# Weight conversion queued behind each attention step, with a fixed order of the first transfers

## The chip, the cores and the metric

The kernel runs on one core of one Trainium2 chip. A core has a matrix engine (PE), three engines that work on vectors (DVE, ACT and POOL), and a queue, SP, that issues transfers (DMAs) between the chip's memory and the on-chip buffers. Each engine takes its instructions strictly in the order in which they stand in its own queue; engines wait for one another by semaphores. The metric is the device time of one execution in microseconds (us), the median of three.

## The reference

Three parts are computed in sequence, all in float32:

```
k_all, v_all = concat(k_g, k_l), concat(v_g, v_l)          # per batch (4) and head (8): 32 global + 512 local rows of 64
out_g = softmax(q_g @ k_all.T / 8) @ v_all
a_l   = softmax(concat(q_l @ k_g.T / 8, where(|i - j| <= 32, q_l @ k_l.T / 8, -1e9)))
out_l = a_l @ concat(v_g, v_l)
x = concat(out_g, out_l) as 2304 tokens x 512
x = x / sqrt(mean(x * x) + 1e-6) * rms_g
x = (silu(x @ w_gate) * (x @ w_val)) @ w_out               # 512 -> 1536 -> 512
h = x @ w_in                                               # 512 -> 2048
out = ((a0 + a1 h + a2 h^2 + a3 h^3) / (1 + |b0||h| + |b1| h^2 + 1e-6)) @ w_out2   # 2048 -> 512
```

The weights arrive as 64-bit floats, which the engines do not compute in.

## The kernel before

**Weights.** A weight tile (512 columns by 128 rows, 512 KB as 64-bit words) is loaded by one DMA (line 66) and turned into two float32 tiles, a rounded high part and the rest, by eight instructions in four stages (`Weights.stages`): ACT at lines 83 and 85, DVE at lines 91, 92 and 95, POOL at line 99, then ACT at line 104 and POOL at line 105. `Weights.step` moves each tile under way by one stage and takes up a new one when fewer than two are under way. The gate, value and output tiles of the first group (g0 to g3, v0 to v3, o0 to o3) are converted while attention runs.

**Attention** runs in 32 steps, one per batch, pair of heads and half of the 512 rows. Step s transposes keys (`make_k`, tile psK) and queries (`make_q`, psQ), multiplies them (`scores`, psS), takes mask and minimum on DVE (tile p), exponentiates on ACT (line 367, tile p), transposes (psT), multiplies with the values (`pv`, psO) and transposes back (psX) into the token tile x. The windows of values, vw, are laid out by two loads from memory and two copies from buffer to buffer (line 278). Keys, queries and values of a step are loaded two to four steps ahead, into buffers that are used in turn (kin0, kin1, qin0, qin1, vw0 to vw3). Every fourth step or so handles the global rows as well (psG, psGT, psOg).

**The first feed-forward block** follows in *units* of 12 matmuls (tiles psg, psv, psA), spread among the attention steps: from step `START` a target of units per step is set, at first 7 units up to step `SECOND`, then up to 60 at the last step. Before a group of tokens is used it is normalized (`norm`, tiles st and x) and split (tile xt).

**What sets the order.** The code is traced in the loop over t in `tile_attn_ffn_kernel`; a scheduler then puts the instructions of each engine in an order from priorities and a model of their times. `tc.issue_after(i)` keeps what is traced inside it behind instruction i on i's engine. Transfers on SP carry one of eight semaphores in turn, so that a DMA is issued when the one eight places ahead has landed.

**In the first five steps** of before, `wts.step` is called four times per t from t = 2. The order in which its instructions and those of attention stand is left to the scheduler. One small instruction belongs to the last part of the kernel: line 918 takes the absolute value of the coefficients b (tile bv) on ACT, and its DMA is issued at t = 3.

Of the kernel before, what the change touches and what calls it, by code (L numbers as in the profile page):

```python
# [134 lines left out]
class Attention:  # L135
# [9 lines left out]
    def __init__(self, tc, pool, x, q_l, k_l, v_l, q_g, k_g, v_g, more):  # L145
        self.tc, self.nc, self.pool, self.x = tc, tc.nc, pool, x
        self.q_l, self.k_l, self.v_l, self.q_g, self.k_g, self.v_g = q_l, k_l, v_l, q_g, k_g, v_g
        nc = self.nc
        self.kin = [pool.tile([128, 4, 2, D], F32, name=f"kin{i}") for i in range(2)]
        self.qin = [pool.tile([128, 2, 2, D], F32, name=f"qin{i}") for i in range(2)]  # L150
        self.gin = pool.tile([128, 2, 2, D], F32, name="gin")
# [22 lines left out]
        self.load_v(0)  # L174
        NEG = -8.0e9
        self.masks = []
        for v in (1, 2, 0):
            m = pool.tile([128, 128], F32, name=f"mask{v}")
            nc.gpsimd.memset(m, 0.0)
            for j in range(4):  # L180
                lo = m[32 * j : 32 * j + 32, 0:96]
                nc.gpsimd.affine_select(
                    out=lo, in_=lo, compare_op=ALU.is_ge, fill=NEG, base=0, pattern=[[1, 96]], channel_multiplier=-1
                )
                nc.gpsimd.affine_select(
                    out=lo, in_=lo, compare_op=ALU.is_ge, fill=NEG, base=2 * WIN, pattern=[[-1, 96]], channel_multiplier=1
                )
            if v == 0:
                nc.gpsimd.memset(m[0:32, 0:32], NEG)
            if v == 2:  # L190
                nc.gpsimd.memset(m[96:128, 64:96], NEG)
            self.masks.append(m)
        self.masks = [self.masks[2], self.masks[0], self.masks[1]]
# [12 lines left out]
        self.load_v(3)  # L206
        self.load_g(0, 1, nc.sync)
# [26 lines left out]

    def load_q(self, s):
        b, hp, u = self.place(s)
        src = self.q_l[b, 2 * hp : 2 * hp + 2, 256 * u : 256 * u + 256]
        if b == 0:
            self.nc.sync.dma_start(
# [3 lines left out]
        else:  # L243
            for hf in range(2):
                self.nc.sync.dma_start(out=self.qin[s % 2][:, :, hf], in_=src[hf].rearrange("(n p) d -> p n d", p=128))

    def load_g(self, b, i, eng):

        g = (self.k_g, self.q_g)[i]
        for hp in range(4):  # L250
            eng.dma_start(
                out=self.gin[32 * hp : 32 * hp + 32, i], in_=g[b, 2 * hp : 2 * hp + 2].rearrange("h j d -> j h d")
            )

    def load_v(self, s):
# [7 lines left out]
        dma = self.nc.sync.dma_start  # L263
# [13 lines left out]
        for p0, w0 in ((0, 0), (64, 2)):  # L277
            dma(out=t[p0 : p0 + 32, :, 1:9], in_=t[32:64, :, w0 : w0 + 8])
# [7 lines left out]

    def load_vn(self, r):
# [3 lines left out]
        self.nc.sync.dma_start(  # L291
# [3 lines left out]
        self.nc.sync.dma_start(out=t[0:32, :, 4], in_=self.v_g[b, 2 * hp : 2 * hp + 2].rearrange("h j d -> j h d"))  # L295
# [30 lines left out]
    def make_g(self, b, i):  # L326
        nc, ps = self.nc, self.bank(1, f"psKG{b}_{i}")
        nc.tensor.transpose(ps[:, 0:128], self.gin[:, i].rearrange("p h d -> p (h d)"), self.ident)
        if i == 0:
            nc.vector.tensor_copy(self.kgt[b % 2], ps[:, 0:128].rearrange("d (p j) -> d p j", p=4))  # L330
            return
        for hf in range(2):
            rows = slice(64 * hf, 64 * hf + 64)
            nc.vector.tensor_copy(
                self.qgz[b % 2][rows, :, 32 * hf : 32 * hf + 32], ps[rows, 0:128].rearrange("d (p j) -> d p j", p=4)
            )

    def scores(self, s):
# [27 lines left out]
        for i in range(4):  # L366
            nc.scalar.activation(out=p[:, i], in_=p[:, i], func=AF.Exp, scale=-1.0, bias=nm[:, i : i + 1])
# [109 lines left out]
    def step(self, t, between):  # L477
# [3 lines left out]
        if t < NS:  # L481
            if i == 0:
# [274 lines left out]
def kernel(  # L757
# [73 lines left out]
    START, SECOND, IN_ATTN = 5, 11, 60  # L831
# [4 lines left out]
    att.set_pools(pp, banks, apool, (3, 2))  # L836
# [5 lines left out]
    for t in range(LAST + 1):  # L842
# [20 lines left out]
        if t >= 2:  # L863
            for _ in range(4 if t < 6 else 2):
# [93 lines left out]
```

## Time and profile before

| | us |
|---|---|
| median of three runs | 1089.58 (1089.46 to 1092.65) |
| the profiled execution | 1092.84 |
| its span, first to last instruction | 1091.1 |
| PE busy in the span | 1007.9 (92%) |
| DVE busy | 792.8 (73%) |
| ACT busy | 600.2 (55%) |
| POOL busy | 373.4 (34%) |

A table of stretches gives the busy time of each engine in each stretch of the span; the difference to its length is the engine's idle time. A list of waits gives, for an engine, what ended its idle time, summed. In a timeline a row has start, duration, engine, line, operation and tiles, and in brackets the idle time ahead of it with what ended it. SPq rows are the issue of DMAs. The page's 40 slices show the granted PE clock below its full value in the first tenth of the span.

### The profile page before, as it was taken

Reading aid. Unit: us, or ns where it says so; the run is one execution under the profiler, and the core shown is the slowest. Engines: PE = TensorE matmul, PEld = TensorE weight load, DVE = VectorE, ACT = ScalarE, POOL = GpSimd, SP = SyncE. Lnnn points to the kernel's source line nnn. Section 1 sums busy time; section 2 is a strip of 40 time slices with the busy share of each in tenths; the row PEclk is TensorE's granted clock in tenths of the full one; section 3 lists DMA queues with packets and bytes.
Section 4 is the critical chain, followed back from the end, with each engine's and each line's share of the span. In section 5 each row is a group of like instructions: output and inputs, shape, how many; then the busy total and the mean of one; then the engine's idle time right before and its main releaser. Section 6 shows DMA issues by size and latency. Waiting matters only on the chain.

```text
span 1091.1 us, 23781 instructions
## 1 busy us (share of the span) xinstructions
PE 1007.9 (92%) x9368; PEld 907.3 (83%) x9368; DVE 792.8 (73%) x1750; ACT 600.2 (55%) x1347; POOL 373.4 (34%) x421
## 2 busy tenths in 40 slices
PE   3669898998989989999999999999999999999997
PEld 2547777877778889899989999888989989898895
DVE  4674554655529999873797453599898998989987
ACT  3644545645447675552654342466666666666675
POOL 5461212212135743220231111354343543435433
PEclk7669999999999999999999999999999999999999
DMA  7943544434116330650430113500000000000000
GB/s 161 276 127 84 114 123 98 108 100 105 32 39 253 117 116 20 212 174 2 155 117 8 33 40 87 185 1 1 30 1 20 11 1 30 1 30 1 1 31 20
DMA packets 104432, 83.46 MB, mean 76 GB/s; under 512 B 63744, under 2 KB 91392, under 8 KB 104320
## 3 DMA queue, kind: packets, MB, share of 16 engines
q1 hardware_dynamic: 102592, 75.64, 23.8%
q0 software_dynamic: 1728, 6.29, 1.8%
q8 instruction: 74, 1.21, 0.5%
q14 instruction: 38, 0.31, 0.1%
HBM read 62.64 MB, written 10.75 MB: 67 GB/s over the span
## 4 chain that ended last, share of the span: by engine, by line
PE 50%; DVE 29%; ACT 8%; DMA 4%; issue 4%; POOL 3%; SPq 2%; ACTq 0%; POOLq 0%; DVEq 0%
PE psg L606 3%; PE psg L608 3%; DVE q L725 3%; PE psS L349 3%; PE psv L608 3%; DVE q L713 3%; PE psv L607 3%; PE psH L703 3%; PE psH L704 3%; PE psv L606 3%; PE psg L607 3%; PE psH L705 3%; PE psB L738 3%; PE psA L633 3%; PE psB L739 3%
## 5 line engine op out<-in xcount | busy, mean ns | idle before, releaser
L130 POOL TENSOR_SCALAR gh<-p 128x384 fp32r<-128x384 f32 (+1 forms) x96 | 58.1, 605 | 210.2 <-DVE p L727 185.8
L703 PE MATMUL psH<-yt,w_h 128*128 128x384 f32 (+1 forms) x384 | 126.0, 329 | 0.9 <-ACT yt L685 0.7
L704 PE MATMUL psH<-yt,w_h 128*128 128x384 f32 (+1 forms) x384 | 125.4, 327 | 0.0
L705 PE MATMUL psH<-yt,w_h 128*128 128x384 f32 (+1 forms) x384 | 123.5, 328 | 0.9 <-DVE yt L686 0.9
L606 PE MATMUL psg<-xt,w_g 128*128 128x288 f32 (+1 forms) x384 | 114.8, 300 | 7.9 <-ACT xt L595 7.9
L633 PE MATMUL psA<-ah,w_o 128*128 128x288 f32 (+1 forms) x384 | 114.3, 299 | 7.6 <-ACT ah L622 3.8
L608 PE MATMUL psg<-xt,w_g 128*128 128x288 f32 (+1 forms) x384 | 114.2, 299 | 5.3 <-DVE xt L596 4.4
L606 PE MATMUL psv<-xt,w_v 128*128 128x288 f32 (+1 forms) x384 | 112.7, 294 | 1.2 <-DVE a L620 1.1
L738 PE MATMUL psB<-w_p,gh 128*128 128x512 f32 x272 | 108.4, 398 | 5.5 <-POOL gh L130 5.4
L607 PE MATMUL psv<-xt,w_v 128*128 128x288 f32 (+1 forms) x384 | 112.0, 292 | 0.0
L635 PE MATMUL psA<-al,w_o 128*128 128x288 f32 (+1 forms) x384 | 111.5, 291 | 0.5 <-DVE al L624 0.4
L608 PE MATMUL psv<-xt,w_v 128*128 128x288 f32 (+1 forms) x384 | 111.8, 292 | 0.0
L634 PE MATMUL psA<-ah,w_o 128*128 128x288 f32 (+1 forms) x384 | 111.6, 291 | 0.0
L607 PE MATMUL psg<-xt,w_g 128*128 128x288 f32 (+1 forms) x384 | 111.5, 291 | 0.0
L729 POOL TENSOR_TENSOR gl<-p,gh 128x384 fp32r<-128x384 f32 (+1 forms) x96 | 108.6, 1131 | 8.0
L739 PE MATMUL psB<-w_p,gh 128*128 128x512 f32 x272 | 107.2, 394 | 0.0
L723 ACT ACTIVATE r<-q,cq 128x384 f32<-128x384 f32 (+1 forms) x96 | 57.4, 598 | 63.4 <-DVE q L713 62.4
L713 DVE SCALAR_TENSOR_TENSOR q<-q,bv,t 128x384 f32<-128x384 f32 (+1 forms) x96 | 68.8, 717 | 21.7 <-ACT q L711 21.6
L621 DVE SCALAR_TENSOR_TENSOR a<-a,psv 128x256 f32<-128x256 f32 (+1 forms) x96 | 41.6, 434 | 56.5 <-ACT a L617 48.2
L606 PEld LDWEIGHTS psg<-xt,w_g 128*128 128x128 f32 x384 | 73.3, 191 | 10.7 <-ACT xt L595 8.9
L633 PEld LDWEIGHTS psA<-ah,w_o 128*128 128x128 f32 x384 | 73.3, 191 | 10.5 <-ACT ah L622 4.5
L740 PE MATMUL psB<-w_p,gl 128*128 128x512 f32 x272 | 82.1, 395 | 0.0
(173 smaller groups left out, 2815.5 us busy)
## 6 DMA issues: line engine op xcount, KB each, us to landing
vw<-vw SPq DMA_DIRECT2D x64, 130.0 KB, 2.5
raw_h<-in_moe_w_in_dram SPq DMA_DIRECT2D x16, 512.0 KB, 3.8
raw_p<-in_moe_w_out_dram SPq DMA_DIRECT2D x16, 512.0 KB, 4.6
raw_g<-in_moe_w_gate_dram SPq DMA_DIRECT2D x12, 512.0 KB, 4.6
raw_v<-in_moe_w_val_dram SPq DMA_DIRECT2D x12, 512.0 KB, 5.9
raw_o<-in_moe_w_out_dram SPq DMA_DIRECT2D x12, 512.0 KB, 6.8
vw<-in_v_l_dram SPq DMA_DIRECT2D x62, 80.0 KB, 2.5
out_dram<-o SPq DMA_DIRECT2D x17, 256.0 KB, 2.0
```

The source lines that it names most:

```text
L606: nc.tensor.matmul(ps, wh, xt[c][:, 0], start=(c == 0), stop=False)
L607: nc.tensor.matmul(ps, wl, xt[c][:, 0], start=False, stop=False)
L608: nc.tensor.matmul(ps, wh, xt[c][:, 1], start=False, stop=(c == 3))
L633: nc.tensor.matmul(ps, wh, ah, start=(i == 0), stop=False)
L634: nc.tensor.matmul(ps, wl, ah, start=False, stop=False)
L635: nc.tensor.matmul(ps, wh, al, start=False, stop=(i == 3))
L703: nc.tensor.matmul(ph[:, :n], wh, yt[:, c, 0, :n], start=(c == 0), stop=False)
L704: nc.tensor.matmul(ph[:, :n], wl, yt[:, c, 0, :n], start=False, stop=False)
L705: nc.tensor.matmul(ph[:, :n], wh, yt[:, c, 1, :n], start=False, stop=(c == 3))
L729: nc.gpsimd.tensor_tensor(out=gl[:, :n], in0=p, in1=gh[:, :n].bitcast(F32), op=ALU.subtract)
L738: nc.tensor.matmul(acc[m], gh[:, sl], wh, start=(k == 0), stop=False)
L739: nc.tensor.matmul(acc[m], gh[:, sl], wl, start=False, stop=False)
```

## The change

- `wts.step` is called 0, 1, 2, 2, 3, 3, 3, 3 times in steps 0 to 7, then twice per step, and in steps 0 to 7 what it issues on ACT and DVE stands behind that step's last exponential and last mask instruction.
- The DMAs that attention issues through `self.dma` are chained in the order of the code in steps 0 to 7. Keys and queries of step 1 and the first weight tile move ahead, the copies of the value windows (`spread_v`) are issued apart from their loads, and the eight small loads of global keys and queries per batch become two.
- One mask is selected on POOL, and the other two are copied from it on DVE.
- `make_g` does global keys and queries in one go, after the queries of the batch's first step.
- Step 8 drains steps 4 to 7 stage by stage, as step 4 does with steps 0 to 3. `SECOND` goes from 11 to 9, the second normalization from t = 10 to t = 8, and the p tile has two buffers for three.

```diff
+        self.order_dma = True
+        self.last_dma = self.last_ttr = self.last_exp = None
         self.load_k(0)
         self.load_q(0)
-        self.load_g(0, 0, nc.sync)
-        make_identity(nc, self.ident)
+        self.load_g(0)
         nc.vector.memset(self.vw[0], 1.0)
         nc.vector.memset(self.vw[1], 1.0)
+        self.load_v(0)
+        self.load_k(1)
+        self.load_q(1)
+        more()
+        self.spread_v(0)
+        self.load_v(1)
+        more()
+        self.spread_v(1)
+        make_identity(nc, self.ident)
...
-        for v in (1, 2, 0):
+        for v in range(3):
             m = pool.tile([128, 128], F32, name=f"mask{v}")
...
+        for v, p0, c0 in ((2, 96, 64), (0, 0, 0)):
+            nc.vector.tensor_copy(self.masks[v], m)
+            nc.vector.memset(self.masks[v][p0 : p0 + 32, c0 : c0 + 32], NEG)
...
-        self.load_k(1)
-        self.load_q(1)
-        self.load_v(1)
-        more()
-        more()
         self.load_v(2)
         self.load_v(3)
-        self.load_g(0, 1, nc.sync)
+
+    def dma(self, out, in_):
+
+        with self.tc.issue_after(self.last_dma.ins) if self.last_dma else nullcontext():
+            d = self.nc.sync.dma_start(out=out, in_=in_)
+        if self.order_dma:
+            self.last_dma = d
...
+    def spread_v(self, s):
+        t = self.vw[s % 4]
+        for p0, w0 in ((0, 0), (64, 2)):
+            self.dma(out=t[p0 : p0 + 32, :, 1:9], in_=t[32:64, :, w0 : w0 + 8])
...
         if t < NS:
-            if i == 0:
-                self.make_g(b, 0)
             if i < 4:
                 self.make_k(4 * b + i)
-            if i == 4:
-                self.make_g(b, 1)
             self.make_q(t)
-        if t == 4:
+            if i == 0:
+                self.make_g(b)
+        if t >= 8:
+            self.order_dma = False
+        if 3 <= t < NS:
+            self.spread_v(t + 1) if t + 1 < NS else None
+        elif t in (0, 1):
+            self.spread_v(t + 2)
+        if t in (4, 8):
             for to in (2, 3, 4):
-                for s in range(4):
+                for s in range(t - 4, t):
                     self.advance(s, to)
+                    between()
...
-    START, SECOND, IN_ATTN = 5, 11, 60
+    START, SECOND, IN_ATTN = 5, 9, 60
...
-    att.set_pools(pp, banks, apool, (3, 2))
+    att.set_pools(pp, banks, apool, (2, 2))
...
-        if t % 4 == 2 and t > 8:
+        if t % 4 == 2 and t > 12:
             norms.append(ffn.norm(ORD[(t - 6) // 4]))
-        elif t == 4:
-            norms.append(ffn.norm(ORD[0]))
+        elif t in (4, 8):
+            norms.append(ffn.norm(ORD[t // 4 - 1]))
...
-        if t >= 2:
-            for _ in range(4 if t < 6 else 2):
+        with ExitStack() as late:
+            if t < 8:
+                late.enter_context(tc.issue_after(att.last_exp.ins))
+                late.enter_context(tc.issue_after(att.last_ttr.ins))
+            for _ in range((0, 1, 2, 2, 3, 3, 3, 3)[t] if t < 8 else 2):
                 wts.step(nc.gpsimd)
```

**Place 1, SP, up to the second load into kin0.** These are the keys of step 2 (raw_g and raw_v are weight tiles; a row with x2 is two DMAs). Before:

```order
L66 DMA raw_g_0_235<-in_moe_w_gate_dram 128x4x256
L278 DMA vw1_101<-vw1_101 32x2x520 x2
L66 DMA raw_v_0_237<-in_moe_w_val_dram 128x4x256
L266 DMA vw2_102<-in_v_l_dram 32x10x64 x2
L282 DMA vw2_102<-in_v_g_dram 32x8x64 x2
L266 DMA vw3_103<-in_v_l_dram 32x10x64 x2
L282 DMA vw3_103<-in_v_g_dram 32x8x64 x2
L278 DMA vw2_102<-vw2_102 32x2x520 x2
L278 DMA vw3_103<-vw3_103 32x2x520 x2
L251 DMA gin_91<-in_q_g_dram 32x2x64 x4
L227 DMA kin0_87<-in_k_l_dram 128x2x256
```

The same place of the change:

```order
L66 DMA raw_g_0_125<-in_moe_w_gate_dram 128x4x256
L214 DMA vw0_100<-vw0_100 32x2x520 x2
L214 DMA vw1_101<-in_v_l_dram 32x10x64 x2
L214 DMA vw1_101<-in_v_g_dram 32x8x64 x2
L66 DMA raw_v_0_133<-in_moe_w_val_dram 128x4x256
L66 DMA raw_g_1_280<-in_moe_w_gate_dram 128x4x256
L214 DMA vw1_101<-vw1_101 32x2x520 x2
L214 DMA vw2_102<-in_v_l_dram 32x10x64 x2
L214 DMA vw2_102<-in_v_g_dram 32x8x64 x2
L214 DMA vw3_103<-in_v_l_dram 32x10x64 x2
L214 DMA vw3_103<-in_v_g_dram 32x8x64 x2
L214 DMA kin0_87<-in_k_l_dram 128x2x256
```

The keys of step 2 were the 39th DMA of the program and are the 30th. The copies of vw2 and vw3 and the query half of gin no longer stand ahead of them, one more weight tile does. The DMA of bv was the 58th and is the 50th.

**Place 2, ACT, ahead of the exponentials of step 3 (p3).** cv, raw and w are weight tiles in conversion, qt and pt attention's own. Before:

```order
L322 ACTIVATE qt3_540<-psQ3_539 128x256
L85 ACTIVATE raw_g_3_503<-raw_g_3_503 128x512
L85 ACTIVATE raw_v_3_505<-raw_v_3_505 128x512
L374 ACTIVATE pt2_552<-psT2_547 128x512
L104 ACTIVATE w_g_2_842<-cv4_652 128x512
L918 ACTIVATE bv_83<-bv_83 128x2
L104 ACTIVATE w_v_2_849<-cv5_661 128x512
L85 ACTIVATE raw_o_0_631<-raw_o_0_631 128x512
L83 ACTIVATE cv6_846<-raw_g_3_503 128x512
L85 ACTIVATE raw_o_1_633<-raw_o_1_633 128x512
L367 ACTIVATE p3_588<-p3_588,nm_108 128x128 x2
L405 ACTIVATE x0_0_70<-psX0_624 128x256
```

The same place of the change:

```order
L83 ACTIVATE cv1_462<-raw_v_0_133 128x512
L85 ACTIVATE raw_v_0_133<-raw_v_0_133 128x512
L331 ACTIVATE qt3_482<-psQ3_481 128x256
L382 ACTIVATE pt2_496<-psT2_491 128x512
L933 ACTIVATE bv_83<-bv_83 128x2
L375 ACTIVATE p3_532<-p3_532,nm_108 128x128 x2
L413 ACTIVATE x0_0_70<-psX0_566 128x256
L375 ACTIVATE p3_532<-p3_532,nm_108 128x128 x2
L104 ACTIVATE w_g_0_577<-cv0_359 128x512
```

The seven conversion instructions between qt3 and p3 are gone from there; the instruction on bv still stands ahead of p3.

**Place 3, DVE, between the masks of step 5 and of step 6** (a1 is the first feed-forward unit's activation, gm the global rows' maximum). Before:

```order
L620 SCALAR_TENSOR_TENSOR a1_0_960<-a1_0_960,psg_1_0_889 128x256
L621 SCALAR_TENSOR_TENSOR a1_0_960<-a1_0_960,psv_1_0_890 128x256
L420 TENSOR_REDUCE gm_110<-psG1_0_978 128x1
L467 COPY x0_0_70<-psGX0_1144 64x2x32 x2
L421 TENSOR_REDUCE gm_110<-psG1_1_979 128x1
L422 TENSOR_REDUCE gm_110<-gm_110 128x1
L423 TENSOR_SCALAR gm_110<-gm_110 128x1
```

The same place of the change:

```order
L91 TENSOR_SCALAR cv5_772<-cv5_772 128x512
L92 TENSOR_SCALAR cv5_772<-cv5_772 128x512
L95 SCALAR_TENSOR_TENSOR cv5_772<-raw_v_2_357,cv5_772 128x512
L632 SCALAR_TENSOR_TENSOR a1_0_875<-a1_0_875,psg_1_0_804 128x256
L633 SCALAR_TENSOR_TENSOR a1_0_875<-a1_0_875,psv_1_0_805 128x256
L428 TENSOR_REDUCE gm_110<-psG1_0_893 128x1
L91 TENSOR_SCALAR cv6_913<-cv6_913 128x512
L475 COPY x0_0_70<-psGX0_1072 64x2x32 x2
L429 TENSOR_REDUCE gm_110<-psG1_1_894 128x1
L92 TENSOR_SCALAR cv6_913<-cv6_913 128x512
L430 TENSOR_REDUCE gm_110<-gm_110 128x1
L95 SCALAR_TENSOR_TENSOR cv6_913<-raw_g_3_455,cv6_913 128x512
```

Before, all twelve tiles (cv0 to cv11) have passed DVE ahead of the masks of step 5; in the change five have (cv0 to cv4), and seven stand among steps 5 to 8 and the first units.

## Rows read from the trace of the kernel before

**Rows 1.** Table of stretches: busy us per engine, granted clock, DMA share, GB/s
```profile
core 0: us, PE busy (x) PEld busy (x) DVE busy (x) ACT busy (x) POOL busy (x), PEclk, DMA share, GB/s
0.00:28.30 28.30, 9.99 (x213) 7.87 (x213) 11.76 (x40) 8.58 (x18) 16.06 (x48) 0.79 0.73 164
28.30:50.70 22.40, 13.37 (x260) 10.89 (x261) 13.91 (x39) 15.17 (x33) 10.21 (x8) 0.65 0.97 283
50.70:76.70 26.00, 15.76 (x214) 10.07 (x213) 20.86 (x51) 14.11 (x35) 16.78 (x14) 0.63 0.59 156
80.00:130.00 50.00, 44.51 (x871) 36.26 (x871) 25.59 (x113) 24.90 (x69) 9.86 (x13) 0.96 0.43 100
130.00:1091.00 961.00, 920.93 (x7778) 839.22 (x7777) 719.46 (x1507) 535.89 (x1191) 317.25 (x335) 0.99 0.21 66
```

**Rows 2.** Waits of PE, whole span: us in total, times, longest
```profile
PE psg L606 <- ACT xt L595: 7.9, 5, 5.1
PE psT L372 <- ACT p L367: 6.7, 1, 6.7
PE psK L304 <- DMA kin<-in_k_l_dram: 5.3, 2, 4.9
PE psQ L304 <- issue: 4.3, 1, 4.3
```

**Rows 3.** Timeline, single rows from 0 to 77 us
```profile
0.74 0.44 SPq L227 DMA_DIRECT2D kin<-in_k_l_dram  x1
...
16.56 0.66 ACT L83 ACTIVATE cv<-raw_g 128x512 f32<-128x512 f32 x1 [7.75 <-DMA raw_g<-in_moe_w_gate_dram]
...
25.38 0.38 SPq L227 DMA_DIRECT2D kin<-in_k_l_dram  x1
...
28.33 1.98 PE L304 MATMUL psK<-ident,kin 128*64 128x128 f32 x16 [4.92 <-DMA kin<-in_k_l_dram]
...
40.08 1.23 SPq L781 DMA_DIRECT2D bv<-in_moe_b_dram  x1
...
44.82 0.19 ACT L918 ACTIVATE bv<-bv 128x2 f32<-128x2 f32 x1
...
50.31 0.39 ACT L367 ACTIVATE p<-p,nm 128x128 f32<-128x128 f32 x1
...
76.70 0.58 PE L606 MATMUL psg<-xt,w_g 128*128 128x256 f32 x1 [5.05 <-ACT xt L595]
```

**Rows 4.** Groups of ACT instructions, 28.3 to 50.7: count, busy us, mean ns
```profile
L367 ACT ACTIVATE p<-p,nm 128x128 f32<-128x128 f32 x8 | 2.8, 389 | 0.0
L85 ACT ACTIVATE raw_g<-raw_g 128x512 int32<-128x512 uint32 x3 | 2.0, 675 | 0.4 <-DMA raw_g<-in_moe_w_gate_dram 0.4
...
L83 ACT ACTIVATE cv<-raw_v 128x512 f32<-128x512 f32 x3 | 2.0, 663 | 0.3 <-DMA raw_v<-in_moe_w_val_dram 0.2
...
L104 ACT ACTIVATE w_g<-cv 128x512 fp32r<-128x512 f32 x2 | 1.2, 623 | 0.0
```

**Rows 5.** Groups of DVE instructions, 50.7 to 76.7
```profile
L91 DVE TENSOR_SCALAR cv<-cv 128x512 f32<-128x512 f32 x5 | 4.1, 818 | 3.4 <-ACT cv L83 3.4
L92 DVE TENSOR_SCALAR cv<-cv 128x512 int32<-128x512 int32 x5 | 3.9, 781 | 0.1
L95 DVE SCALAR_TENSOR_TENSOR cv<-raw_o,cv 128x512 int32<-128x512 int32 x4 | 3.2, 804 | 0.0
```

**Rows 6.** Single lines, 0 to 90 us: ns min/median/max of one instruction
```profile
L91 DVE TENSOR_SCALAR cv<-cv x12: 415/490/1460, 17.2 to 72.4; 128x512 f32<-128x512 f32 x12
...
L92 DVE TENSOR_SCALAR cv<-cv x12: 411/427/1397, 18.4 to 73.1; 128x512 int32<-128x512 int32 x12
...
L95 DVE SCALAR_TENSOR_TENSOR cv<-raw_g,cv x4: 682/693/694, 18.9 to 50.0; 128x512 int32<-128x512 int32 x4
L95 DVE SCALAR_TENSOR_TENSOR cv<-raw_v,cv x4: 676/1180/1779, 21.9 to 52.9; 128x512 int32<-128x512 int32 x4
```

More of the change, by code (lines that the diff above doesn't have):

```diff
@@ L150, in __init__ @@
         self.qin = [pool.tile([128, 2, 2, D], F32, name=f"qin{i}") for i in range(2)]
-        self.gin = pool.tile([128, 2, 2, D], F32, name="gin")
+        self.gin = pool.tile([64, 2 * 4, D], F32, name="gin")
         self.kt = [pool.tile([128, 576], F32, name=f"kt{i}") for i in range(4)]
@@ L173, in __init__ @@
             nc.vector.memset(z, 0.0)
-        self.load_v(0)
         NEG = -8.0e9
         self.masks = []
-        for v in (1, 2, 0):
+        for v in range(3):
             m = pool.tile([128, 128], F32, name=f"mask{v}")
[L179 to L191, printed above, removed]
-            self.masks.append(m)
-        self.masks = [self.masks[2], self.masks[0], self.masks[1]]
+            self.masks.append(m)
+        m = self.masks[1]
+        nc.gpsimd.memset(m, 0.0)
+        for j in range(4):
+            lo = m[32 * j : 32 * j + 32, 0:96]
+            nc.gpsimd.affine_select(
+                out=lo, in_=lo, compare_op=ALU.is_ge, fill=NEG, base=0, pattern=[[1, 96]], channel_multiplier=-1
+            )
+            nc.gpsimd.affine_select(
+                out=lo, in_=lo, compare_op=ALU.is_ge, fill=NEG, base=2 * WIN, pattern=[[-1, 96]], channel_multiplier=1
+            )
+        for v, p0, c0 in ((2, 96, 64), (0, 0, 0)):
+            nc.vector.tensor_copy(self.masks[v], m)
+            nc.vector.memset(self.masks[v][p0 : p0 + 32, c0 : c0 + 32], NEG)
         for vw in self.vw[2:]:
@@ L226, in load_k @@
         if b == 0:
-            self.nc.sync.dma_start(
+            self.dma(
                 out=self.kin[r % 2].rearrange("p n h d -> p (n h d)").rearrange("p (h f) -> p h f", h=2),
@@ L238, in load_q @@
         if b == 0:
-            self.nc.sync.dma_start(
+            self.dma(
                 out=self.qin[s % 2].rearrange("p n h d -> p (n h d)").rearrange("p (h f) -> p h f", h=2),
@@ L244, in load_q, with load_g @@
             for hf in range(2):
[L245 to L253, printed above, removed]
+                self.dma(out=self.qin[s % 2][:, :, hf], in_=src[hf].rearrange("(n p) d -> p n d", p=128))
+    def load_g(self, b):
+        for i, g in enumerate((self.k_g, self.q_g)):
+            self.dma(out=self.gin[32 * i : 32 * i + 32], in_=g[b].rearrange("h j d -> j h d"))
     def load_v(self, s):
@@ L262, in load_v @@
         v = self.v_l[b, 2 * hp]
-        dma = self.nc.sync.dma_start
+        dma = self.dma
         def cut(h0, h1, w0, w1):
@@ L290, in load_vn @@
         t = self.vn[r % 3]
-        self.nc.sync.dma_start(
+        self.dma(
             out=t[:, :, 0:4].rearrange("p h n d -> p h (n d)"),
@@ L324, in make_q, with make_g @@
             self.load_q(s + 2)
-    def make_g(self, b, i):
-        nc, ps = self.nc, self.bank(1, f"psKG{b}_{i}")
-        nc.tensor.transpose(ps[:, 0:128], self.gin[:, i].rearrange("p h d -> p (h d)"), self.ident)
-        if i == 0:
-            nc.vector.tensor_copy(self.kgt[b % 2], ps[:, 0:128].rearrange("d (p j) -> d p j", p=4))
-            return
+    def make_g(self, b):
+        nc, ps = self.nc, self.bank(1, f"psKG{b}")
+        for p in range(4):
+            src = self.gin[:, 2 * p : 2 * p + 2].rearrange("p h d -> p (h d)")
+            nc.tensor.transpose(ps[:, 64 * p : 64 * p + 64], src, self.ident[0:64, 0:64])
+        v = ps[:, 0:256].rearrange("d (p i j) -> d i p j", p=4, i=2)
+        nc.vector.tensor_copy(self.kgt[b % 2], v[:, 0])
         for hf in range(2):
             rows = slice(64 * hf, 64 * hf + 64)
-            nc.vector.tensor_copy(
-                self.qgz[b % 2][rows, :, 32 * hf : 32 * hf + 32], ps[rows, 0:128].rearrange("d (p j) -> d p j", p=4)
-            )
+            nc.vector.tensor_copy(self.qgz[b % 2][rows, :, 32 * hf : 32 * hf + 32], v[rows, 1])
     def scores(self, s):
@@ L366, in scores @@
         for i in range(4):
-            nc.scalar.activation(out=p[:, i], in_=p[:, i], func=AF.Exp, scale=-1.0, bias=nm[:, i : i + 1])
+            self.last_exp = nc.scalar.activation(out=p[:, i], in_=p[:, i], func=AF.Exp, scale=-1.0, bias=nm[:, i : i + 1])
     def trans(self, s):
@@ L496, in step @@
         if t < NS and i == 4 and b + 1 < B:
-            for j in range(2):
-                self.load_g(b + 1, j, self.nc.sync)
+            self.load_g(b + 1)
         if t < NS and i in (3, 4, 5):
```

9 lines of the change are left out of this document (3 added, 6 removed).

## The prediction

> **What bounds the kernel now.** I read the table of stretches first. In 961 us from 130 us on PE is busy for 920.93, with its clock at 0.99 [rows 1]: there the kernel goes at PE's pace. Up to the first feed-forward matmul at 76.70 us [rows 3] PE is busy for 9.99 + 13.37 + 15.76 = 39.1 us and idle for 37.6 [rows 1]. This change works on that beginning. If the first unit comes earlier with the same attention steps done, all that follows can move up by as much, since the later loads are placed by the work ahead of them, not by the time.
>
> The waits of PE name what fills the idle time [rows 2]: the exponentials of step 0, the keys of step 2, a wait of 4.3 us put down to nothing, and the split tokens of the first unit. The timeline shows what is behind them [rows 3]. ACT stood still for 7.75 us in front of a conversion whose weight tile had not landed, with the first exponentials queued behind. The keys of step 2 were issued only at 25.38 us, and PE took them at 28.33. The last exponential of step 3 began at 50.31, and ended at 50.7.
>
> **The change, part by part.** I follow the path to the first unit in three terms, and price the conversions that are put off as a fourth.
>
> *A, the keys of step 2.* The first DMA was issued at 0.74 us and the 39th, these keys, at 25.38 [rows 3]: 38 issues in 24.6 us, 0.65 us each. The change has 29 ahead of them, so 9 x 0.65 = 5.8 us are saved: issue at 19.5, and with the same 2.95 us to their use, 22.5 for 28.33. The transfer engines were at a share of 0.73 in this stretch and 0.97 in the next [rows 1], so there is room for a faster issue. Bounds: no gain, if the bytes ahead (much the same) set the pace, to 5.8. I take 5.8, since the share lies well under the next stretch's. That the exponentials of step 0 no longer wait for a weight tile is worth nothing by itself: steps 0 and 1 then end earlier, and wait for these keys.
>
> *B, from those keys to the exponentials of step 3.* This took 50.7 - 28.3 = 22.4 us, in which ACT ran 18 conversion instructions (6 of line 83, 8 of 85, 4 of 104) at 0.62 to 0.68 us [rows 4], 11.7 us in all, in front of the steps' own work. In the change two are left between the keys and p3, so ACT loses 10.4 us of its queue. Next late is PE itself, with 13.37 us of work in the stretch [rows 1]: 22.5 + 13.4 = 35.9. Later still is bv. Its instruction stands right ahead of p3 on ACT and waits for a DMA that was the 58th and is the 50th. Before, the 19 issues from the keys to bv took 40.08 - 25.38 = 14.7 us, 0.77 each, and its use on ACT came 4.7 us after its issue [rows 3]. Now there are 20: 19.5 + 20 x 0.77 + 4.7 = 39.6. Behind it four exponentials and a copy, some 0.39 each [rows 4], end at 41.6, for 50.7: A and B together give 9.1 us. Bounds: with bv in time 35.9 + 2.0 = 37.9, a gain of 12.8; with bv no earlier than its 44.82 of before, 46.8, a gain of 3.9. I take 9.1, as it goes by the measured pace of issue. So a stall on a DMA is taken away at step 0, and a smaller one put in at step 3.
>
> *C, from there to the first unit.* This took 26.0 us with DVE the busiest, 20.86 [rows 1]. Five tiles were converted in it: 4.1 + 3.9 + 3.2 us and one more of line 95 at 0.68 [rows 5, 6], 11.9 us, 2.4 a tile. The change has three there (cv2 to cv4), 4.8 us less. POOL is next with 16.78 and PE with 15.76, both below DVE's new 16. Bounds 0 to 4.8; I take 4, since DVE was not busy all the time and its waits for ACT (3.4 us [rows 5]) may stay. First unit at 76.7 - 9.1 - 4 = 63.6 us.
>
> *D, the seven tiles put off.* cv5 to cv11 now go through ACT, DVE and POOL among steps 5 to 8 and the first units. On DVE they take 7 x 2.4 = 16.7 us. In 80 to 130 us, where these steps stood, DVE is idle for 50 - 25.59 = 24.4 us, ACT for 25.1 and POOL for 40.1 [rows 1]; so on the sum they are hidden beside PE's 44.51. But each engine goes in order: behind a conversion on DVE stands the next step's mask instruction, for which ACT, then psT on PE wait. Bounds: 0, and 16.7 if every tile lies on the path. I take 3, about one instruction of 0.8 us [rows 5] in front of the masks of each of four steps: near the covered end, since the idle time is half as much again as the need.
>
> A rule of the Trainium skill speaks against this term. The longest instances of the three DVE lines are 1.46, 1.40 and 1.78 us, three times the shortest of the first two [rows 6]. The page "SBUF — State Buffer", section "Who interferes with whom", says that DVE and GpSimd (POOL) share one pair of buffer ports under an exclusive lock, so that certain DVE instructions and a POOL instruction exclude each other for a whole instruction; the trace's spread agrees in kind. If every moved instruction met POOL, a tile would take 4.64 us and the seven 32.5, 8.1 more than DVE's idle time, and the sum would come to 1084.6. By the rows, 2.4 us a tile was measured with POOL busy for 16.78 of 26.0 us; in 80 to 130 us it is busy for 9.86 of 50 before the seven tiles are added, so I keep 2.4.
>
> *The rest* I cost at 0, plus or minus 2 us. The masks on POOL (24 selections, now 8) and the two copies end long before step 2's keys, the cover of all that is shortened ahead of them. With two p buffers the mask of step t writes what psT of t - 2 has read, and psT of t - 1 stands ahead on PE. The joint buffer of global keys and queries is refilled four steps after its use. The copies of vw are issued at least one step ahead of their use. `SECOND` and the second drain move units within attention: there are still 60 by its end, in a stretch in which PE is busy for nine tenths of the time.
>
> **Sum.** -9.1 - 4 + 3 = -10.1 us. The profiled execution took 1092.84 us, its span of 1091.1 and 1.7 around it: 1082.7. It lies 3.3 us above the median of the runs, 1089.58, against which the forecast is 1079.5. Its own range, with B from 3.9 to 12.8 and D up to 8, is 1073 to 1086.
>
> **Rivals.**
> 1. *The loads come no earlier.* The transfers are then the limit from the start: keys at 28.33, bv at 44.8, p3 done at 46.8. For it: a share of 0.97 from 28.3 us on, and the same bytes ahead. Against it: 0.73 before. Gain 3.9 + 4 - 3 = 4.9, or 4 with C a little less: 1085.5.
> 2. *DVE becomes the bound, and the kernel is slower.* In steps 5 to 8 every tile stands in front of a mask that PE waits for, and the units wait for tiles converted last (o3 ahead of psA). Price 16.7 us in place of 3: 1089.6 - 13.1 + 16.7 = 1093. It turns slower from 13.1 / 7 = 1.9 us a tile on the path, against 2.4 measured on the engine. For it: place 3, where conversions are cut in between the first unit's activation and the global maximum. Against it: 24.4 us of idle DVE.
> 3. *All of it is saved.* bv lands by 35.9 and nothing of D shows: 12.8 + 4.8 = 17.6, 1072. For it: eight DMAs fewer ahead of bv. Against it: DVE would then fill its idle time without one step waiting.
> 4. *The change doesn't do what it says*, since a unit needs its weights at once and PE waits for POOL's last stage instead of attention. The order has w_g1 and w_v1 on ACT ahead of the first unit's activation, so I see this for single tiles only, within D.
>
> **Chances.** Forecast 0.58, rival 1 0.16, rival 2 0.12, rival 3 0.14. For this kernel a difference under 0.3%, 3.3 us, can't be told from none. Forecast and rival 3 are faster but for a hundredth or two; of rival 1 two thirds are faster and the rest the same; of rival 2 three quarters slower, the rest the same, and I move 0.02 to each for the orders that shift later. That makes 0.78 faster, 0.11 the same, 0.11 slower. The range of 8 in 10 reaches over rival 1 and to the near side of rivals 2 and 3: 1071 to 1089.
>
> **What the profile of the changed kernel would show.** A: the second load into kin0 issued at 19 to 21 us, psK of step 2 at 22 to 24. B: ACT idle for 2 to 5 us in front of bv, which starts at 38 to 41; p3 done by 43. C: the first psg at 61 to 67, PE idle for some 25 us until then in place of 37.6. D: DVE busy for more than 0.75 of the 45 us from there on, PE still over 0.85, first psA some 10 us ahead of before. From there on the same PE work as before.
>
> The prediction is wrong if the keys of step 2 still come at 28 (A), if bv stalls ACT beyond 44 (B), or if PE is idle for more than 8 us between the first unit and the first psA (D).

## The result and the profile after

The changed kernel takes 1080.91 us (median of 4 runs, 1078.59 to 1081.57), the kernel before 1089.62 beside it: ratio 0.991, interval [0.9886, 0.9933]. In a second set of runs it was 1080.37 us, 0.9902 [0.9882, 0.9922]. The profiled execution took 1080.32 us with a span of 1078.5, so 12.5 us less than the one of before, which lay 3.2 us above its median. One run of keys_bv (1875 us) and one of vn_early (2785 us), far slower than all others, are left out of the medians below.

I cut each span at two events: the start of the first unit (first psg) and of the last attention output (last psX). Kernel before:

```profile
core 0: us, PE busy (x) PEld busy (x) DVE busy (x) ACT busy (x) POOL busy (x), PEclk, DMA share, GB/s
0.00:76.70 76.70, 39.12 (x685) 28.83 (x685) 46.53 (x129) 37.86 (x84) 43.04 (x70) 0.69 0.75 196
76.70:321.70 245.00, 227.53 (x3976) 187.51 (x3977) 124.96 (x509) 120.72 (x332) 51.03 (x65) 0.97 0.37 86
321.70:1091.10 769.40, 741.20 (x4708) 690.98 (x4707) 621.26 (x1113) 441.66 (x933) 279.36 (x286) 1.00 0.18 61
```

The changed kernel, at the same events:

```profile
0.00:62.80 62.80, 33.40 (x688) 24.60 (x688) 31.18 (x112) 26.20 (x65) 19.98 (x37) 0.80 0.84 222
62.80:307.30 244.50, 227.59 (x3995) 189.28 (x3995) 135.87 (x530) 130.81 (x352) 69.69 (x79) 0.96 0.39 91
307.30:1078.50 771.20, 741.83 (x4696) 692.34 (x4694) 625.07 (x1113) 440.56 (x932) 278.30 (x286) 0.99 0.18 61
```

Nearly all of the gain is ahead of the first unit: 13.9 us there, 0.5 in the second stretch, and 1.8 lost in the third. (Twelve matmuls of a unit, psA, stand in the second stretch now and stood in the third before.) Of the 13.9, 8.2 are idle time of PE (37.6 to 29.4) and 5.7 are PE's busy time: the same matmuls ran at a granted clock of 0.80 in place of 0.69 (a mean over its two levels, 2.4 GHz, which counts as 1, and 1.2 GHz, which counts as 0.5).

Another execution of the same program, from the second set of runs, shows how much of a span is the clock's:

```profile
0.00:61.60 61.60, 32.73 (x687) 23.91 (x687) 30.96 (x112) 26.12 (x65) 19.90 (x36) 0.80 0.86 227
61.60:303.10 241.50, 222.97 (x3994) 185.24 (x3995) 135.98 (x530) 130.68 (x352) 70.09 (x79) 0.99 0.39 92
303.10:1074.50 771.40, 738.99 (x4696) 688.37 (x4696) 625.01 (x1113) 441.23 (x932) 280.65 (x286) 1.00 0.18 61
```

It is 4.0 us shorter with the same instructions in the same order. In the second stretch PE is idle longer (18.5 for 16.9 us) but busy for 4.6 us less, at 0.99 for 0.96. So from here on a stretch is read as idle plus busy, with the clock beside it.

Single rows of the changed kernel, which answer to [rows 3]:

```profile
19.83 0.40 SPq L214 DMA_DIRECT2D kin<-in_k_l_dram  x1
...
22.88 1.98 PE L313 MATMUL psK<-ident,kin 128*64 128x128 f32 x16 [9.29 <-DMA kin<-in_k_l_dram]
...
35.22 0.62 SPq L793 DMA_DIRECT2D bv<-in_moe_b_dram  x1
...
40.16 0.20 ACT L933 ACTIVATE bv<-bv 128x2 f32<-128x2 f32 x1 [7.55 <-DMA bv<-in_moe_b_dram]
...
41.12 0.68 ACT L375 ACTIVATE p<-p,nm 128x128 f32<-128x128 f32 x2
...
62.76 0.58 PE L618 MATMUL psg<-xt,w_g 128*128 128x256 f32 x1 [3.13 <-ACT xt L607]
```

The keys of step 2 are issued 5.5 us earlier. ACT now stands still for 7.55 us in front of bv. PE's longest waits over the whole span, for [rows 2], are those for step 2's keys and for ACT behind bv, where a copy into x stands among the exponentials. In front of the keys PE now stands for 9.3 us, where it stood for 4.9: they come earlier, but what is ahead of them ends earlier still.

```profile
PE psK L313 <- DMA kin<-in_k_l_dram: 13.9, 4, 9.3
PE psT L380 <- ACT x L413: 7.6, 2, 5.9
```

### The profile page after: what moved, and what is told of

It is laid out like the page before. It is cut to its first block, busy times and chain, and to the rows that moved or that the text cites. A ratio compares the mean times of both kernels' runs of the same rounds, so it can differ in the third digit from the quotient of the medians.

```text
span 1078.5 us, 23732 instructions
## 1 busy us (share of the span) xinstructions
PE 1002.8 (93%) x9376; PEld 906.2 (84%) x9376; DVE 792.1 (73%) x1754; ACT 597.6 (55%) x1347; POOL 368.0 (34%) x401
## 4 chain that ended last, share of the span: by engine, by line
PE 38%; DVE 15%; ACT 4%; DMA 2%; issue 2%; POOL 2%; ACTq 0%; POOLq 0%; SPq 0%; DVEq 0%
PE psH L715 4%; PE psH L717 4%; PE psB L750 4%; PE psH L716 4%; PE psB L751 4%; PE psB L752 3%; DVE q L725 2%; PE psg L620 2%; DVE q L737 2%; DVE r L738 2%; PE psg L618 2%; PE psg L619 2%; PE psv L618 2%; PE psv L620 2%; PE psv L619 2%
## 5 line engine op out<-in xcount | busy, mean ns | idle before, releaser
L645 PEld LDWEIGHTS psA<-ah,w_o 128*128 128x128 f32 x384 | 73.2, 191 | 12.5 <-ACT ah L634 3.8
```

The lines of the kernel that those rows point to most:

```text
L645: nc.tensor.matmul(ps, wh, ah, start=(i == 0), stop=False)
```

## The experiments

Twelve kernels in three sets of four, in the order of the table, each set on another chip beside the kernel before (1090.90, 1089.71 and 1090.26 us). The changed kernel ran in the first set alone, so across sets the ratio is the fairer measure. "First unit" and "stretch", the time from first unit to last attention output, come from one profiled execution of each kernel.

| kernel | median us | ratio to before, interval | first unit | stretch |
|---|---|---|---|---|
| changed, again | 1080.37 | 0.9902 [0.9882, 0.9922] | 61.6 | 241.5 |
| bv_late | 1081.94 | 0.9912 [0.9891, 0.9933] | 65.6 | 244.5 |
| keys_early | 1082.96 | 0.9931 [0.9909, 0.9952] | 64.2 | 246.8 |
| keys_bv | 1088.27 | 0.9971 [0.9953, 0.9988] | 64.7 | 250.9 |
| no_tie | 1086.35 | 0.9968 [0.9947, 0.9988] | 64.8 | 252.7 |
| cnt_before | 1094.66 | 1.0044 [1.0025, 1.0062] | 71.1 | 250.1 |
| d_skip | 1076.40 | 0.9875 [0.9848, 0.9902] | 62.4 | 238.8 |
| vn_bv | 1075.76 | 0.9866 [0.9836, 0.9895] | 60.1 | 244.3 |
| units_before | 1094.38 | 1.0043 [1.0029, 1.0057] | 61.4 | 255.9 |
| fill | 1081.49 | 0.9907 [0.9889, 0.9924] | 63.2 | 247.5 |
| vn_early | 1079.22 | 0.9896 [0.9875, 0.9917] | 61.4 | 244.2 |
| raw_vn_bv | 1073.18 | 0.9845 [0.9831, 0.9860] | 56.1 | 243.8 |

**Terms A and B: are the keys and bv on the path?** My theory was that they are, one behind the other. The changed kernel as the measure:

> The changed kernel as it is, as the measure for the three kernels run beside it. Theory (the time goes with the beginning: pace of the loads, then bv, then the first unit; all later work follows): 1080.9 us again, plus or minus 1.5, first unit at 62.8 us. Rival (the profile's 12.5 us are partly a chance of the one execution of before): the ratio to the kernel before comes out nearer 1 than 0.991.

bv_late:

```diff
-    nc.scalar.activation(out=bv, in_=bv, func=AF.Abs)
     with tc.issue_after(ffn.last_silu.ins):
+        nc.scalar.activation(out=bv, in_=bv, func=AF.Abs)
```

> One instruction of ACT is moved, the Abs of the b coefficients, from ahead of step 3's exponentials to the end of the first feed-forward; its DMA stays. In the trace of the changed kernel the masks of step 3 end on DVE at 35.1 us and ACT stands still for 7.55 us until bv at 40.2. Theory: p3 begins at 35.2 in place of 40.3 and is done at 36.7 (41.8); the first unit comes at 58 (62.8), since the later loads and weight tiles don't bind; total 4 to 5 us less than the changed kernel. Rival 1 (another load comes just behind bv, such as step 5's query at 41.5 us, or the weight tiles): p3 at 35 but first unit at 61 to 62 and total within 1.5 us of the changed kernel. Rival 2 (the beginning is given back in steps 5 to 8, where seven tiles wait): first unit at 58, total the same.

keys_early (keys_bv is this and bv_late):

```diff
-        self.load_v(2)
-        self.load_v(3)
...
-        elif t in (0, 1):
-            self.spread_v(t + 2)
+        elif t == 1:
+            for s in (2, 3):
+                self.load_v(s)
+            for s in (2, 3):
+                self.spread_v(s)
```

> The keys and queries of steps 2 and 3 are issued ahead of the eight value loads of vw2 and vw3: keys of step 2 as the 22nd DMA (30th), of step 3 as the 25th or so (35th); bv stays the 50th, and in front of step 3's exponentials. Theory (the pace of issue sets the keys, bv sets p3): keys of step 2 issued at 15.4 us (19.8), used at 18.5 (22.9); p3 still at 40 to 41 behind bv, first unit at 62 to 63, total within 1.5 us of the changed kernel: term A is worth nothing as long as bv stands there. Rival (the keys are on the path and bv is only waited for because of what follows): p3 and first unit 4 us earlier, total 4 us less. Rival (the transfers and not the issues set the pace): keys used at 21 to 23 all the same.

> Both edits: keys and queries of steps 2 and 3 ahead of the values, and bv's Abs moved away. Theory: keys of step 2 used at 18.5 us and of step 3 at 22.6, masks of step 3 done at 29.4 (35.1), p3 done at 31 to 32, first unit at 53 to 56, total 7 to 10 us less than the changed kernel. Rival 1 (from some point the weight tiles or the later loads bind): first unit at 58 as with bv moved alone, total 4 to 5 us less. Rival 2 (given back later): first unit early, total no less than the changed kernel's.

My theory fell with bv_late. Step 3's exponentials came at 36.9 us (40.3), and the first unit 2.8 to 4 us later than in the changed kernel; total the same. About 2 us of this lateness are not the edit's: in this execution the keys of step 2 were issued at 21.91 us (19.83 and 20.00 in the changed kernel), ahead of anything that the edit touches. Without these 2 us the first unit would still come no earlier. Waits of PE in bv_late, 0 to 65.6 us:

```profile
PE psK L313 <- DMA kin<-in_k_l_dram: 15.0, 3, 10.7
PE psQ L313 <- DMA qin<-in_q_l_dram: 7.2, 2, 6.2
...
PE psOg L452 <- DMA vn<-in_v_l_dram: 3.1, 1, 3.1
```

What bv no longer hides, two other loads take: step 5's query, and the second load into vn, which the global output needs. That output stands on DVE ahead of the normalization of the first unit's tokens. On SP's queue of bv_late one sees why vn is late; the last line is from the list of SP's own waits:

```profile
48.77 1.16 SPq L214 DMA_DIRECT2D vw<-in_v_l_dram  x2
50.84 0.38 SPq L214 DMA_DIRECT2D qin<-in_q_l_dram  x1
53.25 1.24 SPq L214 DMA_DIRECT2D vw<-vw  x2
...
58.28 0.45 SPq L214 DMA_DIRECT2D vn<-in_v_l_dram  x1
...
SPq L214 <- DMA vw<-in_v_l_dram: 2.0, 1, 2.0
```

The copy vw<-vw stood in the queue for 2.0 us until its own load had landed, and the issue of vn stood behind it and six more loads. In keys_early the keys of step 2 were issued some 4 us earlier but used at 20.7 us, 2.2 earlier and not 4.4: this is near the rival (21 to 23), by which the transfers set the pace. bv came at 40.5, as the theory had it, while the first unit at 64.2 is 1.4 to 2.6 later than in the changed kernel. In keys_bv PE waited 8.7 us for the query and 3.3 for vn, and no expectation was met: the total is 7.9 us longer than the changed kernel's, though its first unit is only 1.9 to 3.1 later. The rest lies in its second stretch, in PE's busy time, at a low clock:

```profile
64.70:315.60 250.90, 232.29 (x3994) 192.18 (x3995) 134.78 (x530) 130.70 (x352) 69.67 (x79) 0.94 0.37 88
```

So in these four kernels neither bv nor the keys by themselves set the time of the first unit. I took it that the stream of loads does, in the order in which SP issues it.

**vn_early, vn_bv and raw_vn_bv** test this. In the first two the second vn load is issued behind the first (vn_bv is on bv_late):

```diff
-        if t < NS and i in (3, 4, 5):
+        if t < NS and i in (3, 4, 5) and t != 4:
             self.load_vn(4 * b + i - 3)
+        if t == 3:
+            self.load_vn(1)
```

> The second load into vn is issued right behind the first, as in the best kernel so far, but bv's Abs stays ahead of step 3's exponentials. Theory (two limits of nearly the same time, bv on ACT and the load of vn, of which each hides the other): first unit at 61 to 62.5 us (62.8 and 61.6), for only 0.8 us of PE's wait for vn can go; total within 1.5 us of the changed kernel. Rival (the vn load alone was the limit): first unit at 59 to 60.5 as in the kernel with both, total 3 to 5 us less.

> Over the kernel with bv's Abs moved away, the second load into vn is issued right behind the first, ahead of a copy of vw1 that waits for its own load. In the kernel with bv moved, p3 came 3.4 us earlier than in the changed kernel (36.9 for 40.3) but the first unit 2.8 later (65.6): PE waited 6.2 us for step 5's query and 3.1 for vn, and DVE 4.2 us with the normalization queued behind the global output. Theory (the stream of loads, in its order on SP, sets the time of the first unit): PE no longer waits for vn, DVE's 4.2 us go, first unit at 61 to 62.5. Rival (some other thing holds the first unit back): first unit at 64 to 66 again. Total, from either: within 3 us of the changed kernel, since two profiles of that differ by 4 us with the granted clock (0.973 and 0.984).

raw_vn_bv, on vn_bv:

```diff
-        for _ in range(2):
-            if loads:
-                loads.pop(0)()
+        with tc.issue_after(att.last_dma.ins) if t in (3, 4) else nullcontext():
+            for _ in range(2):
+                if loads:
+                    loads.pop(0)()
```

> Over the kernel with bv's Abs moved and vn's second load ahead (1075.8 us, first unit at 60.1): the four output weight tiles are loaded behind the keys, query and vn loads of steps 3 and 4, not ahead of them. PE waited 5.9 us for step 5's query there, whose DMA stood behind three of those tiles. Theory (stream of loads): PE waits under 1 us for that query, first unit at 54 to 57, total 2 to 6 us less than 1075.8. Rival (something else holds the first unit back, such as the two late steps on DVE): first unit at 59 to 60, total the same. Rival (output tiles now come late): first unit earlier, first psA no earlier than 111.8, total the same.

The first unit came as the stream has it in all three, in vn_bv a little earlier. Each limit alone is worth nothing that shows (bv_late and vn_early within 1.6 us of the changed kernel), both together bring the first unit to 60.1, and with the output tiles behind the query it comes at 56.1. The total of vn_bv lies 4.6 us under the changed kernel's, more than the 3 us expected and more than its first unit explains (1.5 to 2.7 us); the intervals overlap, so this difference is not shown. PE's waits in vn_bv, and the same wait in raw_vn_bv:

```profile
PE psQ L313 <- DMA qin<-in_q_l_dram: 6.8, 2, 5.9
```

```profile
PE psQ L313 <- DMA qin<-in_q_l_dram: 1.1, 1, 1.1
```

raw_vn_bv is the best version, 7.2 us under the changed kernel by the medians and some 6 by the ratios, and the intervals don't overlap. What it gains is ahead of the first unit, and part of it is given back: beside the execution of the changed kernel at the same mean clock (0.984, the one that starts its units at 61.6) 5.5 us are won there, 3.5 are lost behind it, and the span is 2.0 us shorter.

```profile
0.00:56.10 56.10, 31.62 (x687) 23.72 (x687) 32.03 (x112) 26.23 (x64) 20.10 (x36) 0.87 0.90 229
56.10:299.90 243.80, 226.21 (x3995) 188.58 (x3995) 135.49 (x530) 130.66 (x352) 70.09 (x79) 0.97 0.41 96
```

**Terms B and C: the conversions.** no_tie takes the tie away, cnt_before keeps it with the counts of before:

```diff
-            if t < 8:
-                late.enter_context(tc.issue_after(att.last_exp.ins))
-                late.enter_context(tc.issue_after(att.last_ttr.ins))
```

> The weight conversions are no longer tied behind the attention steps; order of DMAs, masks, units and step counts stay as in the changed kernel. All twelve tiles are then converted ahead of the first unit, in place of five, and bv stands between the exponentials of step 3. Theory 1 (B and C: conversions on ACT and DVE are on the path to the first unit): DVE has up to 7 x 2.4 = 16.7 us more ahead of it, about half of it hidden by its idle time: first unit at 68 to 74 us (62.8 and 61.6 in two profiles of the changed kernel), DVE idle for less than 20 of these; total 2 to 6 us over the changed kernel, since steps 5 to 8 then have no tiles. Theory 2 (the stream of loads sets the time of the first unit, by the second load into vn): its issue at 54 to 56 us and the first unit at 61 to 64 as before, total within 2 us of the changed kernel.

```diff
-            for _ in range((0, 1, 2, 2, 3, 3, 3, 3)[t] if t < 8 else 2):
+            for _ in range((0, 0, 4, 4, 4, 4, 2, 2)[t] if t < 8 else 2):
```

> The conversion stages keep their tie, but as many stand behind each step as in the kernel before: none behind steps 0 and 1, four behind each of steps 2 to 5. Seven tiles are then on ACT ahead of the first unit (five in the changed kernel). Theory 1 (each tile costs its 2.4 us of DVE on the path): first unit 3 to 5 us later, 66 to 68 us, and what follows shorter by less: total 0 to 3 us over the changed kernel. Theory 2 (stream of loads): first unit at 61 to 64, total within 2 us.

Neither theory had both numbers of either kernel. With ten of the twelve tiles through DVE ahead of it (the last two end just behind) the first unit of no_tie comes only 2.0 to 3.2 us later, while that of cnt_before comes 8.3 to 9.5 later with eight. So it does not go by the number of tiles. What differs in the traces is how long DVE stands in front of a tile that ACT hasn't begun, with the masks queued behind. This wait of DVE from 30 to 72 us, in the kernel before, the changed one, no_tie and cnt_before:

```profile
DVE cv L91 <- ACT cv L83: 9.5, 4, 3.4
```
```profile
DVE cv L91 <- ACT cv L83: 2.0, 2, 1.2
```
```profile
DVE cv L91 <- ACT cv L83: 2.9, 4, 1.3
```
```profile
DVE cv L91 <- ACT cv L83: 13.2, 5, 6.5
```

The first units came at 76.7 (71.2 without the 5.5 us by which the keys were later), 62.8, 64.8 and 71.1 us: late in the two kernels with the long waits. That the waits are the cause is read from the traces; no run changes them alone. In cnt_before the longest, 6.5 us, ends at 42.4 us, and ACT itself stood in front of bv (5.7 us) and of a tile on POOL (1.4 us) in that time. Both kernels lose again in the second stretch, by PE's busy time (233.7 and 233.8 us for 223.0 and 227.6), at a clock of 0.94 and 0.95. This is no_tie, in an execution that lies 3.6 us above its median:

```profile
0.00:64.80 64.80, 35.86 (x687) 26.68 (x688) 41.99 (x130) 36.68 (x83) 35.03 (x47) 0.74 0.86 221
64.80:317.50 252.70, 233.74 (x3994) 192.28 (x3995) 125.44 (x512) 120.81 (x334) 54.89 (x68) 0.94 0.36 87
```

**Term D.** d_skip leaves DVE's part of the seven tiles out:

```diff
+            if not 5 <= num <= 11:
                 nc.vector.tensor_scalar(out=vf, in0=vf, scalar1=TINY, ...
```

> The seven tiles put off (cv5 to cv11) leave out their three DVE instructions (16.7 us on DVE), so the weights they give are not the reference's; ACT's and POOL's parts stay. This prices term D. Forecast's term: DVE's part of the tiles costs 3 us, so total 3 us less than the changed kernel, and first psA some 3 us earlier against the first unit. Rival (the tiles lie on the path): 8 to 16 us less. Rival (the tiles are hidden, and what is lost after the first unit is lost to a low clock): within 1.5 us of the changed kernel, and the granted clock of 65 to 110 us no higher.

```profile
62.40:301.20 238.80, 223.72 (x3995) 186.03 (x3995) 122.68 (x509) 130.20 (x352) 66.86 (x78) 0.99 0.39 93
```

At the same clock of 0.99 the stretch is 2.7 us shorter than the changed kernel's 241.5, PE idle for 15.1 us in place of 18.5; in total 4.0 us by the medians, with intervals that overlap. The 8 to 16 us of the rival are out. In the changed kernel the seven tiles took 14.7 us on DVE, 2.1 a tile, the parts of L95 the most:

```profile
L95 DVE SCALAR_TENSOR_TENSOR cv<-raw_o,cv 128x512 int32<-128x512 int32 x4 | 4.3, 1073 | 0.1
L92 DVE TENSOR_SCALAR cv<-cv 128x512 int32<-128x512 int32 x7 | 4.2, 596 | 0.1
L91 DVE TENSOR_SCALAR cv<-cv 128x512 f32<-128x512 f32 x7 | 2.9, 421 | 0.1
L95 DVE SCALAR_TENSOR_TENSOR cv<-raw_g,cv 128x512 int32<-128x512 int32 x1 | 1.7, 1659 | 0.0
L95 DVE SCALAR_TENSOR_TENSOR cv<-raw_v,cv 128x512 int32<-128x512 int32 x2 | 1.6, 816 | 0.0
```

**The rest.** units_before puts the units' places back:

```diff
-        if t in (4, 8):
+        if t == 4:
...
-    START, SECOND, IN_ATTN = 5, 9, 60
+    START, SECOND, IN_ATTN = 5, 11, 60
...
-        if t % 4 == 2 and t > 12:
+        if t % 4 == 2 and t > 8:
             norms.append(ffn.norm(ORD[(t - 6) // 4]))
-        elif t in (4, 8):
+        elif t == 4:
             norms.append(ffn.norm(ORD[t // 4 - 1]))
```

> Only the placing of the units in attention is put back: SECOND = 11, the second drain of four steps at t = 8 taken out, the norms at t = 4 and then at t = 10, 14, ... as in the kernel before. This prices the part that the forecast cost at 0 plus or minus 2. By two profiles at the same granted clock (0.94 and 0.95 in the 70 us from the first unit on) the stretch from the first unit to the last attention output took 245.0 us in the kernel before and 241.5 in the changed one, though that has seven tiles more in it, worth 2.7 us by the kernel that leaves out their DVE part (238.8). Theory (the placing of the units gives 6 us): this stretch 247 to 249 us, total 4 to 7 us over the changed kernel's 1080.4 to 1080.9. Rival (the forecast's 0): the stretch 241 to 245, total within 2 us.

It costs 14.0 us, as much as cnt_before and twice the most that the theory had. The whole gain is lost, though the first unit comes at 61.4:

```profile
0.00:61.40 61.40, 34.24 (x688) 24.77 (x688) 30.82 (x112) 26.34 (x65) 19.91 (x37) 0.82 0.87 229
61.40:317.30 255.90, 237.98 (x3983) 192.69 (x3983) 136.74 (x530) 130.50 (x351) 70.03 (x79) 0.94 0.37 87
317.30:1092.30 775.00, 742.08 (x4708) 694.36 (x4706) 620.04 (x1113) 441.42 (x933) 279.92 (x286) 0.99 0.18 61
```

PE's idle time in the second stretch is 17.9 us, as in the changed kernel (16.9 and 18.5); its busy time is 10.4 to 15.0 us more. Busy time times clock is 223.7 us here, and 218.5 and 220.7 in the two executions of the changed kernel, each good to about 1.2 us with a clock of two digits, so most of it is the clock and some 3 to 5 us are not. The lower clock is not the chance of one execution: the median granted clock is 0.974 over the six runs of the changed kernel here, 0.969 over the six of units_before and 0.968 over the twelve of no_tie. Why this order gets it stays open; the kernel before places its units by the same settings, and its stretch took 245.0 us at 0.97.

**fill** asks whether the clock follows idle time:

```diff
+        if qd == 0:
+            for _ in range(7):
+                nc.tensor.matmul(ps[:, 256:512], self.ident, self.qgz[0].rearrange("d p j -> d (p j)"), start=True, stop=True)
```

> Seven matmuls of 128x256 elements, whose result nobody reads, are put on PE between the first global output and the first unit, where PE stood idle for 3.1 us in the changed kernel. Theory (the low clock at the units' start follows PE's idle time ahead of it): the granted clock of the 10 us from the first unit on rises from 0.66 and 0.76 (two profiles) to 0.85 or more, the stretch from first unit to last attention output is 1 to 3 us shorter, total 0 to 2 us less. Rival (what lowers the clock isn't this idle time, but the work before it or chance): clock 0.6 to 0.8 as before, total the same or up to 1 us more.

Here are ten-us stretches from the first unit on, in fill and then in the changed kernel:

```profile
63.20:73.20 10.00, 9.31 (x145) 7.08 (x143) 6.42 (x24) 6.01 (x16) 3.05 (x4) 1.00 0.20 48
73.20:83.20 10.00, 10.00 (x188) 8.44 (x187) 7.62 (x25) 6.97 (x17) 6.96 (x7) 1.00 0.11 26
83.20:93.20 10.00, 10.00 (x62) 6.76 (x62) 2.03 (x8) 1.75 (x4) 3.56 (x3) 0.63 0.21 48
```

```profile
62.80:72.80 10.00, 10.00 (x111) 8.14 (x112) 5.09 (x17) 5.70 (x14) 5.87 (x7) 0.72 0.36 86
72.80:82.80 10.00, 9.20 (x132) 7.81 (x131) 5.17 (x21) 3.81 (x12) 4.29 (x4) 0.83 0.01 2
82.80:92.80 10.00, 9.36 (x128) 6.25 (x126) 5.58 (x14) 5.39 (x12) 6.35 (x5) 1.00 0.30 71
```

The clock at the start rose from 0.72 (0.84 in the other execution of the changed kernel) to 1.00, as the theory had it, but ten us on it fell to 0.63, with PE busy throughout. The stretch was 247.5 us and the total the same: the theory fell on both. It is one execution, and the extra matmuls write the bank of the first global output, for which DVE waited 2.2 us, so the total is not the price of the clock alone.

## Why the prediction was right, and where it was not

The time was right by 1.4 us, and the first unit at 62.8 us by 0.8 (63.6). Not every step under it was.

- **A held in time.** Keys issued at 19.83 (19.5), used at 22.88 (22.5): 5.5 us for 5.8. Rival 1 is out. But keys_early shows that transfers bound too: a further 4.2 us at the issue gave 2.2 at the use, and none at the first unit.
- **B held in time, not as a cause.** bv came at 40.16 (39.6) and step 3's exponentials ended at 41.8 (41.6). ACT's idle time was 7.55 us and not 2 to 5, as the masks of step 3 were done at 35.1. I took bv for the path; bv_late shows that the query and vn were due just behind it. The 9.1 us came out right (8.9) because bv is one of the same stream of loads, whose pace of issue I had measured.
- **C came out 5.0 us for 4**, from 41.8 to 62.8. DVE was busy for 15.34 us there in place of 20.86, near the 16 forecast. I let DVE's waits for ACT stay; in C they went from 3.4 to 2.0 us, and from 9.5 to 2.0 between 30 and 72 us. By no_tie and cnt_before the number of tiles alone doesn't set the first unit; that the waits do is likely and not shown.
- **D was 2.7 to 4.0 us for 3**, from one profile and from medians whose intervals overlap. By the Trainium skill's rule ("SBUF — State Buffer", section "Who interferes with whom") my estimate was 8 us more than DVE's idle time, with every instruction excluded by POOL; the trace's 2.1 us a tile, not 4.64, and d_skip do not bear that estimate out. One sign of D was wrong: DVE was busy for 0.61 of the 45 us from the first unit on (27.31), not over 0.75. The first psA came at 114.7 and 110.5, 5 and 10 us earlier than the 120.1 of before, and not 10 in both. PE was idle for 6.3 and 7.9 us until then, just under the 8 that would have spoken against D.
- **The rest was not 0.** This is the step that failed. I wrote that the units' places don't matter as there are 60 of them by the end of attention anyway. Without them the kernel takes 1094.38 us: rival 2's time, by another mechanism. With this a premise of the sum fails too, that all that follows moves up with the first unit. In units_before it comes 15.3 us earlier than before (61.4 for 76.7), but the second stretch is 10.9 us longer and the third 5.6. The sum came out right because the change makes both moves: two errors cancelled, and that is luck. `SECOND`, the second drain and the norms were put back together, so which of the three counts is not known; the one mask and the joint buffer were not tested.
- **PE's busy time was taken as fixed.** I forecast 25 us of idle time ahead of the first unit; it was 29.4, and what was missing was made up by 5.7 us less of busy time, at a higher clock. The third stretch's 1.8 us were not forecast either.

The rows behind C (from the last exponential of step 3 to the first unit) and D (the 45 us from there on) in the changed kernel:

```profile
41.80:62.80 21.00, 13.01 (x217) 8.28 (x216) 15.34 (x45) 14.12 (x36) 11.36 (x11) 0.74 0.78 211
62.80:107.80 45.00, 40.12 (x539) 30.60 (x539) 27.31 (x84) 24.71 (x59) 24.74 (x22) 0.82 0.26 61
```

Against the medians the change gave 8.7 to 10.5 us for 10.1. The 13.9 us of the beginning are from two single executions, of which that of before was 3.2 us slower than its median; in which stretch a typical execution of it is shorter is not shown.

## What to carry to other kernels

Before a wait is taken away, list the loads due just behind it on the same queue: each of two limits alone was worth nothing here, both together brought the first unit forward by 1.5 to 2.7 us, and with the bulky loads moved behind them by 5.5 to 6.7. When work is moved between engines, look where a queue will stand in front of it, and not only at its sum: the kernel with eight tiles ahead of the first unit was later than the one with ten. And read each stretch as idle plus busy with its clock: with PE at nine tenths, an order can lose in busy time what it won in idle time, as units_before did.

## What was not expected of the hardware

Two executions of one program differed by 4.0 us of span, 4.6 of them in PE's busy time between the same two events, at a mean clock of 0.96 and 0.99. The clock also fell with PE fully busy: to 0.63 in ten us in which PE was busy for 10.00, after twenty at 1.00 (fill). PE's busy time over the whole span times the mean clock was 975.8 and 978.8 us in the changed kernel, 976.6 before and 980.8 in units_before. So spans that differ by 18 us (1074.5 to 1092.3) hold, by this estimate, the same work to within 5 us.
